# A hand-written order of 994 named operations is replaced by another order of the same operations (attention into a Hyena convolution, one core)

## The chip, the cores and the metric

The kernel runs on one core of one Trainium2 chip. The metric is the device time of one execution in microseconds (us), the median of several runs. TensorE (PE) does the matmuls, VectorE (DVE), ScalarE (ACT) and GpSimd (POOL) the rest; SyncE (SP) issues most of the transfers.

## The reference

Four batches, eight heads, 768 positions, head size 64. Three heads attend causally over everything; the other five see only the first 4 keys and the last 64. The attention's output, 768 x 512 for each batch, is projected to three parts; the middle one is convolved over the sequence with a filter (a circular convolution through a real FFT), multiplied by the other two, and projected once more.

```python
a = softmax(where(mask, q @ k.T / 8, -1e9))        # per batch and head
x = (a @ v) laid out as (4, 768, 512)
x1, x2, x3 = split(x @ w_proj, 3)                  # each (4, 768, 512)
x2_conv = irfft(rfft(x2) * rfft(filter_fft))       # over the 768 positions
return (x1 * x2_conv * x3) @ w_out
```

## The kernel before

The heads are taken in 16 pairs, n = 0 to 15, four for each batch b. All intermediate results stay in SBUF; the Fourier transforms are matmuls with tables of cosines and sines that the kernel makes at its start. Every step is a small function with a name, and the whole program is written out in one string, FAST: the functions are called in the order in which their names stand there. A scheduler does not move anything. So FAST fixes the order of the instructions on every engine; each engine works through its own list, and waits where data is missing.

A word of FAST is a name, then (for some) `/v`, `/s` or `/p`, the engine that does it (VectorE, ScalarE, GpSimd), then (for TensorE's) `@0` to `@3`, which of four PSUM buffers of two banks it writes:

```python
for word in FAST.split():
    name, _, slot = word.partition("@")
    name, _, eng = name.partition("/")
    now.update(slot=slot, engine=eng)
    ops[name]()
```

The names that matter here, with their lines:

- For a pair n: `lq`, `lk`, `lv` load q, k and v (L905, L927); `cq`, `ck` or, from pair 8 on, `cqk` cast to bf16 (L535 on VectorE, L537 on GpSimd, L541 on ScalarE); `T` transposes q and k into `qkT`, on TensorE for pairs 0 to 7 (L952, with the eviction `E`) and by a DMA that SyncE issues from pair 8 on (L962); `ks` copies the sink keys into the windowed heads' rows.
- `sc` are the scores (L990; contraction over the 64 rows of one head), `sb` adds masks in PSUM for the first four pairs (L1001), `ex` the exponentials on ScalarE (L1007), `mk` masks afterwards, `at` attention times v (L1050), `rec` and `nm` the normalisation on VectorE (L1056, L1067). `tn`/`te` transpose the result on TensorE (L1123) for pairs 0 to 10; from 11 on a DMA does it (L1132).
- `fd`, `fe`, `fA`, `fS`, `fb`, `fr` add and subtract the attention's thirds and halves (L544, L1095), `W` is the first half of the Fourier transform (L1103 to L1111) with its eviction `We`.
- For a batch b: `X` projects in the frequency domain (L1154), `Xe` evicts, `pa`, `pb`, `pc` multiply with the filter's spectrum, `c` is the inverse transform (L1227), `cv` its butterflies (L1238), `x1` and `x3` the two other projections (L1189), `g` and `y` the gating, `o` the output projection (L1262; the last tile in halves at L1257), `oe` its eviction, `st` the store.
- Once: `lfilt` loads the filter (L776, a DMA that GpSimd issues), `lw` and `lwo` the weights (L784, L789), `fold0` and `fold1` fold the filter (L793, L797), `F` transforms it (L805), `H` scales its spectrum out of PSUM.
- At the end: `chk` compares the head pattern with the expected one, `gd0` to `gd4` check on all rows that the softmax sums are sane, with one 1-column matmul, `gd3` (L669), and write one number, `other` (L674). The last line of the program reads `other` on all engines and branches to a general version if it isn't zero. `rest` is eight matmuls whose result nobody uses (L586). `late` is a two-element copy of the last output tile (L579).

The transfers have queues: SyncE issues its DMAs one after the other in FAST's order, and stops at one whose buffer or data isn't ready; GpSimd does the same with `lfilt`, `lw` and `lwo` between its computing instructions.

Of the kernel before, what the change touches and what calls it, by code (L numbers as in the profile page):

```python
# [64 lines left out]
ck1/p blank2@3 ones0 E0.0/v cq1/p btab lq3 gs1/v gs0/p sc0.0@0 sc0.5@2 gc/p cq2/p sc0.2@3 sb0.5 sb0.0 ck2/p ex0.5
sb0.2 kz0/v T1.1@1 gs2/p T1.0 E1.0/v sc0.4@2 ex0.2 sb0.4 ex0.0 blank1@3 sc0.1@3 E1.1/v sc0.3@0 ones2 lk3 sb0.3 ex0.4
lv2 cv0/p T2.0@1 lv3 sb0.1 kz2/p ex0.3 ex0.1 T2.1 gr0/v ones1 sc1.1@2 sb1.1 sc1.0@0 lk5 E2.1/v ex1.1 ck3/p gm0.2
sb1.0 cq3/p E2.0/s at0.0@3 at0.1 ks1/v lq5 gm1.2 sc2.1@2 Gk0 sc2.0@1 lfilt ex1.0 gm1.1 gm0.1 sb2.0 sb2.1 Gt0@0 rec0
cv1/s nm0/v ex2.0 lw1.1 Ge0/v Gt1@3 sc1.2@1 ex2.1 ks2/s vs1/v Gh0 sb1.2 vx1/s sc2.4@0 ex1.2 T3.0@2 T3.1 lq4 Ge1/v lk4
fd0/v E3.0/v lw1.0 ex2.4 lq6 sc2.3@3 at1.1@1 fe0/v sc2.2@0 at1.0 E3.1/v rec1 sb2.2 nm1/v ex2.3 W0.1@3 cv2/s cv3/p  # L70
vx3/s ex2.2 fe1/v tn0@2 W0.0 te0/s sc3.1@1 sb3.1 vx2/v fd1/v at2.0@0 ck5/p vs2/s sc3.0@2 at2.1 We0/v lv4 cq5/s ks3/s
T5.1@3 cq4/p sb3.0 T5.0 ex3.1 sc3.2@1 sb3.2 rec2 nm2/v fe2/p E5.0/v ck4/p E5.1/v ex3.0 Gh1 W1.0@0 lv5 ex3.2 T4.0@2
E4.0/s W1.1 tn2@1 lq7 vs3/v tn1@3 We1/s T4.1 te2/v sc5.0@1 sc5.1@0 lk6 te1/v at3.1@3 fold1 at3.0 E4.1/s fold0 rec3
# [15 lines left out]
x11.0.1@2 fr6 x11.0.0 T9 oe0.3/s at8.0@1 at8.1 lq11 fS7/v fA7/v oe0.1/s fr7 xs1.0/s chk cv9/v vx9/v sc9.1@0 fb6/p
fb7/v rec8 T10 lv10 nm8/v fe8/p sc9.0@3 x11.3.1@2 x11.3.0 W7.1@1 ex9.1 W7.0 W6.0@0 fd8/p ks9/p ex9.0 xs1.3/v W6.1  # L90
sc10.4@3 sc10.3@2 cqk11/p We6/v mk9.1 vs9/s We7/s sc10.0@1 lv11 ex10.4 ex10.3 sc9.2@3 mk9.0 ex9.2 X1.1.1@0 mk9.2 T11
tn8@2 X1.1.0 fS8/v ex10.0 Xe1.1/s X1.2.0@3 at9.1@1 te8/s at9.0 sc10.1@0 ks10/p X1.2.1 fA8/v ex10.1 Xe1.2/s sc11.0@2
rec9 sc11.1@0 cv10/v cv11/p nm9/v st0.1 x31.0.1@1 mk10.1 lk12 ex11.0 fd9/p ex11.1 x31.0.0 X1.0.1@3 lq12 sw1.1 lv13
ks11/v pa1.1/p sc10.2@2 vx10/s sc11.2@0 X1.0.0 g1.0 sw1.0 vs10/v vs11/v ex10.2 x11.2.0@1 pb1.1/v fe9/v lq14 Xe1.0/s
mr10 fb8/v mk10.0 fS9/v mk10.2 x11.2.1 o0.4.0@2 mk11.1 ex11.2 tn9@3 xs1.2/s at10.0@0 at10.1 mk11.0 lq13 mk11.2 fA9/v
x11.1.0@1 x11.1.1 o0.5.0 o0.4.1 o0.5.1 fb9/p vx11/s rec10 cqk12/s nm10/v at11.0@0 at11.1 fr9 te9/s fr8 fd10/p
x31.1.0@3 T12 oe0.5/s W9.1@2 W9.0 xs1.1/s pb1.2/v x31.1.1 rec11 nm11/v tn10@1 pc1.1/v We9/s W8.1@0 tn11 W8.0 te10/s
g1.1 pa1.0/v sc12.1@2 pa1.2/v sc12.4@3 x31.2.1@1 x31.2.0 We8/s sc12.0@0 fe10/v pc1.2/v fe11/p ex12.1 x12.0.0@2 g1.2
fS10/p fA10/p lk13 ex12.4 x12.0.1 ex12.0 x32.0.0@3 pb1.0/v lv12 fb10/p pc1.0/v xs2.0/s sc12.5@1 sc12.2@0 fd11/v
sc12.3@2 x32.0.1 ex12.5 c1.0.0@1 c1.0.1 ex12.2 fr10 fA11/v lq15 fS11/v W10.1@0 W10.0 ex12.3 fr11 c1.1.0@2 c1.1.1  # L100
fb11/p g2.0 ce1.0/s c1.2.0@3 We10/s ce1.1/s W11.0@0 cv1.0.1 cv13/p cv1.0.0 mk12.1 cv1.1.0 cv1.1.1 c1.3.1@1 cqk13/s
W11.1 c1.3.0 y1.1/v y1.0/v ce1.3/v lk14 We11/s c1.2.1 ce1.2/s cv1.3.0 X2.1.0@2 lk15 T13 cv1.3.1 cqk14/s cv1.2.1
cv12/s X2.0.0@0 X2.1.1 mk12.0 X2.0.1 x31.3.0@1 T14 mk12.2 Xe2.1/s x31.3.1 Xe2.0/s cv1.2.0 y1.3/v sc13.1@3 vs13/s
ex13.1 sc13.0@2 g1.3 cqk15/p at12.1@0 at12.0 pa2.0/p sc14.1@1 rec12 sc14.0@3 ex13.0 nm12/v vx13/s X2.2.0@2 y1.2/v
ks13/s X2.2.1 pb2.0/v o1.1.0@0 ex14.1 pa2.1/v T15 lv15 mk13.1 o1.1.1 ex14.0 sc13.2@1 sc15.0@3 mk13.0 pc2.0/v ks14/p
Xe2.2/s fe12/v ex13.2 sc15.1@2 mk13.2 o1.0.0 st0.5 ex15.0 o1.0.1 x12.3.0@1 pa2.2/v x12.3.1 pb2.1/v at13.1@3 ex15.1
at13.0 ks15/p tn12 oe1.1/s fd12/v rec13 xs2.3/s lv14 exp0 o1.4.0@2 o1.5.0 fS12/v sc14.4@0 nm13/v sw2.1 fA12/v
sc15.2@1 fe13/v sc14.3@3 fd13/v st0.3 ex14.4 sc14.2@0 ex15.2 o1.4.1 ex14.3 o1.5.1 x12.2.1@1 mk14.1 fS13/v fr12 ex14.2
# [1290 lines left out]
```

## Time and profile before

| | |
|---|---|
| median of 3 runs | 183.8 us (183.39 to 184.66) |
| span of the profiled execution | 182.1 us |
| what lies around the span, by the median | 1.7 us |
| TensorE busy | 172.8 us (95%) |
| VectorE busy | 149.8 us (82%) |
| ScalarE busy | 145.3 us (80%) |
| GpSimd busy | 77.5 us (43%) |
| DMA | 33.8 MB, 186 GB/s on average |

The profile's span begins with the first instruction and ends with the last. "Busy" for TensorE is the time in which at least one matmul is in flight; a matmul that starts a little late because its operands came late still counts as busy. The profiled execution has no time of its own beside its span: the 1.7 us is the median of the runs less the span.

### The profile page before, as it was taken

What the parts mean: (1) busy time and instruction counts of PE and PEld (TensorE: products, weight loads), DVE (VectorE), ACT (ScalarE), POOL (GpSimd) and SP (SyncE); (2) the same over time, 40 slices, a digit from 0 to 9 for tenths busy, and PEclk for the clock granted to TensorE, in tenths of its full rate; (3) what the DMA queues carried; (4) which work ended last, traced back from release to release, by engine and by line L of the source; (5) the groups of instructions that cost most, each with busy time, mean ns of one, the idle gap of its engine ahead of it and who ended that gap; (6) DMA issues with size and microseconds to landing.
All of it is one profiled execution on the core that took longest, in us unless ns stands there. A gap on an engine that the chain in (4) does not pass through costs nothing.

```text
span 182.1 us, 4374 instructions
## 1 busy us (share of the span) xinstructions
PE 172.8 (95%) x1684; PEld 103.6 (57%) x1700; DVE 149.8 (82%) x298; ACT 145.3 (80%) x196; POOL 77.5 (43%) x94
## 2 busy tenths in 40 slices
...
GB/s 159 356 203 287 294 257 200 204 290 230 232 224 166 184 228 198 116 214 142 265 217 200 150 231 166 123 208 243 228 153 112 184 0 0 58 2 119 127 277 184
DMA packets 78396, 33.83 MB, mean 186 GB/s; under 512 B 67618, under 2 KB 74786, under 8 KB 78370
## 3 DMA queue, kind: packets, MB, share of 16 engines
...
q14 instruction: 12, 0.10, 0.2%
...
## 4 chain that ended last, share of the span: by engine, by line
PE 82%; DVE 8%; ACT 4%; DMA 3%; issue 1%
PE f_x_ps L1189 23%; PE f_X_ps L1154 12%; PE f_out_ps L1262 10%; PE f_c_ps L1227 9%; PE f_sc L990 8%; PE f_att L1050 7%; DMA f_qkT<-f_qk_bf 3%; PE f_qkT_ps L952 2%; PE f_sc L1001 2%; PE warm L454 2%; PE f_xt_ps L1123 2%; ACT f_pT L1007 1%; DVE f_HAB L691 1%; PE f_W_ps L1103 1%; PE f_W_ps L1105 1%
## 5 line engine op out<-in xcount | busy, mean ns | idle before, releaser
L1007 ACT ACTIVATE f_pT<-f_sc 128x1024 bf16<-128x1024 f32 (+3 forms) x68 | 58.5, 914 | 3.6 <-PE f_sc L990 2.0
L1189 PE MATMUL f_x_ps<-f_xT,f_wproj 128*128 128x384 bf16 x256 | 46.9, 326 | 0.0
L1189 PEld LDWEIGHTS <-f_wproj 128*128 128x128 bf16 x256 | 23.9, 98 | 17.4 <-issue 1.6
L990 PE MATMUL f_sc<-f_qkT 64*128 64x128 bf16 (+3 forms) x328 | 20.9, 242 | 2.4 <-DMA f_qkT<-f_qk_bf 1.4
L1154 PE MATMUL f_X_ps<-f_wproj,f_xh 128*128 128x512 bf16 x90 | 22.1, 379 | 0.6 <-issue 0.2
L544 POOL TENSOR_TENSOR f_fo<-f_attn 128x384 bf16<-128x384 bf16 x15 | 14.6, 990 | 18.4 <-DVE f_attn L1067 17.3
L1262 PE MATMUL f_out_ps<-f_wout,f_gy 128*128 128x512 bf16 x86 | 22.0, 379 | 0.3
L990 PEld LDWEIGHTS <-f_qkT 64*128 64x128 bf16 x328 | 11.4, 94 | 13.0 <-issue 7.9
L1238 DVE TENSOR_TENSOR turns<-angle,f_c_ps 128x384 bf16<-128x384 f32 x32 | 16.3, 550 | 2.6 <-ACT angle L541 1.3
L1227 PE MATMUL f_c_ps<-f_Gi,f_P 128*128 128x384 bf16 x96 | 18.2, 326 | 0.1
L1050 PEld LDWEIGHTS <-f_pT 128*128 128x128 bf16 x472 | 16.2, 97 | 2.4 <-issue 0.4
L1050 PE MATMUL f_att<-f_v_aug,f_pT 128*128 128x65 bf16 x392 | 17.0, 193 | 0.0
L541 ACT COPY f_o<-f_out_ps 128x1024 f32<-128x1024 f32 (+2 forms) x15 | 12.1, 818 | 6.2 <-PE f_out_ps L1262 5.1
L541 ACT CAST f_X<-f_X_ps 128x1024 bf16<-128x1024 f32 x12 | 12.1, 1016 | 4.9 <-PE f_X_ps L1154 4.9
L1067 DVE TENSOR_TENSOR f_attn<-f_att,f_recs 128x768 bf16<-128x768 f32 x16 | 15.1, 951 | 0.6
L544 POOL TENSOR_TENSOR f_P<-f_X,f_HAB 128x1024 bf16<-128x1024 bf16 x4 | 8.9, 2215 | 14.5 <-ACT f_X L541 14.5
L544 POOL TENSOR_TENSOR f_gy<-turns,f_gy 128x768 bf16<-128x768 bf16 x5 | 8.5, 1710 | 14.6 <-DVE turns L1238 14.6
L1154 PEld LDWEIGHTS <-f_xh 128*128 128x128 bf16 x96 | 8.9, 97 | 10.2 <-issue 0.5
L1262 PEld LDWEIGHTS <-f_gy 128*128 128x128 bf16 x92 | 8.5, 98 | 8.8 <-POOL f_uv L544 0.4
L541 ACT COPY angle<-f_c_ps 128x384 f32<-128x384 f32 x15 | 7.2, 478 | 7.7 <-PE f_c_ps L1227 5.4
L1227 PEld LDWEIGHTS <-f_P 128*128 128x128 bf16 x96 | 9.1, 98 | 6.0 <-issue 0.2
L537 POOL CAST f_qk_bf<-qk_ahead 128x768 bf16<-128x768 f32 (+1 forms) x9 | 8.0, 900 | 8.7 <-DMA qk_ahead<-in_k_dram 3.4
...
## 6 DMA issues: line engine op xcount, KB each, us to landing
...
```

What stands on the lines that cost most here:

```text
L537: nc.gpsimd.tensor_copy(out=out, in_=in_)
L541: nc.scalar.copy(out=out, in_=in_)
L544: (nc.gpsimd if now["engine"] == "p" else nc.vector).tensor_tensor(out, a, b, op)
L990: nc.tensor.matmul(sc[:, bank, col:col + 128 * cnt], lhsT=keys, rhs=qkT(n)[rows, 0, 128 * i:128 * (i + cnt)], start=(col == 0 or not biase ...
L1007: nc.scalar.activation(out=pT(n)[:, c, :, 0:w], in_=held[f"sc.{n}.{c}"][:, :, 0:w], func=AF.Exp, scale=SCALE)
L1050: nc.tensor.matmul(att[:, hh, 65 * i:65 * i + 65], lhsT=pT(n)[:, c, bank, col:col + 128], rhs=values, start=(z == 0), stop=(z == len(here) ...
L1067: nc.vector.tensor_mul(attn(n).rearrange("p i hh d -> p hh i d"), rows[:, :, :, 0:64], recs()[:, n][:, :, :, None].to_broadcast([128, 2, N ...
L1154: nc.tensor.matmul(ps[:, u, :], lhsT=xh(b)[:, cc, chain, 128 * part:128 * part + 128], rhs=wproj()[:, cc, DM:2 * DM], start=(cc == 0), sto ...
L1189: nc.tensor.matmul(ps[:, s, 0:HS], lhsT=wproj()[:, cc, part * DM + cb * 128:part * DM + (cb + 1) * 128], rhs=xT(b)[:, cc, s * HS:s * HS + HS],
L1227: nc.tensor.matmul(ps[:, r, 0:HS], lhsT=P(b)[:, t, u, ch], rhs=Gi()[:, tile_no], start=(m == 0), stop=(m == 2))
L1238: fn(conv[:, half * HS:half * HS + HS], held[f"evs.{b}.{cb}"], held[f"c_ps.{b}.{cb}"][:, 1, 0:HS])
L1262: nc.tensor.matmul(ps[:, i % 2, :], lhsT=gy(b)[:, cb, i * 128:(i + 1) * 128], rhs=wout()[:, cb, :], start=(cb == 0), stop=(cb == NC - 1))
```

## The change

FAST is replaced by another sequence of the same 994 words' names. No function, tile, constant or matmul is added or taken away. Three things differ: the order of the names, the engine letters of some of them, and the PSUM buffer numbers of some. The first line of the table, before and after, and the last:

```diff
-mtab3 lq2 lk2 wrap0 size blank3@0 sin1 ck0/v lv0 T0.1@1 E0.1/s kz1/v sin2 cq0/p cos2 blank0@2 alt cos1 T0.0 lv1 gr1/s
+ck0/s wrap0 mtab3 blank2@0 size lq2 cos2 blank3@0 sin2 T0.1@2 E0.1/v sin1 blank1@3 cos1 alt gc/v gr0/v ones2 btab
...
-o3.2.0@3 o3.2.1 o3.3.0@2 oe3.1/s o3.3.1 oe3.4/v st3.0/v oe3.2/s oe3.3/s o3.5.1@1 st3.4/v st3.1/v oe3.6/s o3.5.0@0
-oe3.5/s st3.6/s st3.2/v st3.3/v st3.5/v rest@3 late
+oe3.4/v st3.6/s st3.4/v oe3.2/v st3.2/v oe3.5/s o3.3.0@0 o3.3.1 gd0 gd1 gd2 late oe3.3/s st3.5/v rest@2 chk st3.3/v
+gd3@1 gd4
```

Counted by kind, the engine letters move `ce` (inverse transform's eviction) from 15 on ScalarE and 1 on VectorE to 10 and 6, `oe` from 15 and 1 to 12 and 4, `te` from 7 and 4 to 5 and 6, the copies `vx` from 8 on ScalarE to 4 (4 now on GpSimd), `cqk` from 6 on ScalarE to 4, and the casts `cv` of v from 7 on VectorE, 5 on GpSimd, 4 on ScalarE to 3, 10 and 3. The filter's `H` go from 4 on VectorE and 5 on ScalarE to 6 and 3. Of the casts of q and k in the first stage `cq1`, `ck1`, `ck3`, `cq3`, `cq4` go from GpSimd and `cq5` from ScalarE to VectorE. TensorE's list alternates between `sc` and other work 76 times before and 70 times after.

Three places, engine by engine. The first is GpSimd around the load of the filter (`f_filt`), some 17 to 24 us into the program. Before:

```order
L537 CAST f_v_aug_177<-f_v_f_0_139 128x12x64
L880 MEMSET f_v_x_270 64x520
L884 MEMSET f_v_aug_281 128x12
L537 CAST f_qk_bf_307<-qk_ahead_66 128x768 x2
L776 DMA f_filt<-in_moe_filter_fft_dram 128x6x512
L784 DMA f_wproj<-in_moe_w_proj_dram 64x4x512 x2
L537 CAST f_v_aug_177<-f_v_f_3_265 128x12x64
```

and after:

```order
L880 MEMSET f_v_x_418 64x520
L537 COPY f_qkT_292<-f_qkT_292 64x4x4
L776 DMA f_filt<-in_moe_filter_fft_dram 128x6x512
L537 COPY f_v_x_166<-f_v_aug_162 64x4x65
L537 CAST f_v_aug_194<-f_v_f_3_370 128x12x64
L537 COPY f_qkT_497<-f_qkT_497 128x4x4
L537 COPY f_v_x_418<-f_v_aug_194 4x520
L544 TENSOR_TENSOR f_fo_584<-f_attn_576 128x384
L537 CAST f_qk_bf_541<-qk_ahead_69 128x768
L784 DMA f_wproj<-in_moe_w_proj_dram 64x4x512 x2
```

The filter's load stood behind two casts of pair 3's q and k; it now stands behind the sink copy of pair 2 (`ks2`, the copy within `f_qkT_292`), which must wait until TensorE has made the scores `sc2.0` and `sc2.1`. The first two weight loads (`lw1.0`, `lw1.1`) stood right behind the filter's and now come six instructions later.

The second is SyncE's list around the transpose of pair 12 (`f_qkT_12`), about 98 us into the program. Before and after:

```order
L1179 DMA f_Xw_1_1719<-f_X_1_2_1671 64x1024
L908 DMA f_qk_f32_14_1762<-in_q_dram 128x6x64 x2
L908 DMA qk_ahead1_69<-in_q_dram 128x6x64 x2
L962 DMA_TRANSPOSE f_qkT_12_1885<-f_qk_bf_12_1848 128x12x128
L1132 DMA_TRANSPOSE f_xT_2_1645<-f_attn_11_1905 128x6x128
```

```order
L927 DMA f_v_f32_13_1799<-in_v_dram 128x6x64 x2
L962 DMA_TRANSPOSE f_qkT_12_1822<-f_qk_bf_12_1765 128x12x128
L908 DMA qk_ahead0_66<-in_q_dram 128x6x64 x2
L908 DMA qk_ahead1_69<-in_q_dram 128x6x64 x2
L1132 DMA_TRANSPOSE f_xT_2_1664<-f_attn_11_1904 128x6x128
```

The load of pair 13's q (the row into `qk_ahead1`) stood in front of this transpose; it now stands behind it, with pair 15's between. The cast that feeds the transpose (`cqk12`) goes from ScalarE to VectorE.

The third is the end of VectorE's list. Before and after, from the last gating on:

```order
L1219 TENSOR_TENSOR f_gy_2676<-turns,f_x_ps_3_2832 128x384
L674 TENSOR_SCALAR other<-f_rows_right,differ 1x1
L535 COPY f_o_2_2883<-f_out_ps_4_2855 128x512
L579 CAST f_sane<-f_o_2_2883 1x2
L1314 TENSOR_LOAD other
```

```order
L535 COPY f_o_1_2879<-f_out_ps_2_2862 128x512
L655 TENSOR_SCALAR f_sane<-f_recs 128x192
L660 SCALAR_TENSOR_TENSOR f_sane<-f_recs,f_sane 128x192
L665 TENSOR_REDUCE f_right<-f_sane 128x1
L579 CAST f_sane<-f_o_2_2874 1x2
L642 MEMSET want 1x8
L645 MEMSET want 1x1 x3
L646 TENSOR_SCALAR zeros<-flags 1x16
L648 TENSOR_TENSOR local<-zeros 1x8
L649 TENSOR_TENSOR differs<-local,want 1x8
L650 TENSOR_REDUCE differ<-differs 1x1
L674 TENSOR_SCALAR other<-f_rows_right,differ 1x1
```

The checks (`gd0` to `gd2`, `chk`, `gd4`) stood earlier in the program and `other` was written before the last output tiles; they now stand behind the last evictions. On TensorE `gd3`, whose result `gd4` reads, stood in front of batch 3's output projection; it now is the last matmul of all, behind the eight of `rest`.

More of the change, by code (lines that the diff above doesn't have):

```diff
@@ L63 @@
 FAST = """
-mtab3 lq2 lk2 wrap0 size blank3@0 sin1 ck0/v lv0 T0.1@1 E0.1/s kz1/v sin2 cq0/p cos2 blank0@2 alt cos1 T0.0 lv1 gr1/s
[L65 to L73, printed above, removed]
@@ L89 @@
[L89 to L98, printed above, removed]
@@ L99 @@
[L99 to L108, printed above, removed]
@@ L114 @@
-fS14/p fA14/p x32.3.1@0 cv2.0.0 x13.1.1@2 fA15/p ce2.2/s x13.1.0 g2.2 x32.3.0 xs3.1/s fr14 fb15/v y2.0/v fb14/v
-W14.0@3 W14.1 x13.0.1@2 We14/s cv2.2.0 fr15 x13.0.0 W15.0@3 W15.1 cv2.2.1 x33.0.1@1 We15/v x33.0.0 y2.2/p X3.2.1@3
-X3.2.0 xs3.0/s Xe3.2/s X3.1.1@2 y2.3/v g3.0 X3.1.0 X3.0.1@1 sw3.1 g2.3 Xe3.1/s sw3.0 X3.0.0 x13.2.1@0 pa3.1/v Xe3.0/s
-o2.1.0@3 x13.3.0@2 o2.0.0 pa3.2/p x33.2.0@1 x13.2.0 pb3.1/p x13.3.1 pb3.2/v gd0 pc3.2/v o2.1.1 xs3.2/s pa3.0/v
-pb3.0/v x33.2.1 x33.1.0@0 pc3.1/v o2.0.1 xs3.3/s g3.2 c3.0.0@2 pc3.0/p x33.1.1 c3.1.0@1 oe2.1/s ce3.0/s o2.4.0@3 g3.1
@@ new lines @@
+kz2/v cq0/s T0.0 E0.0/s lk2 sc0.3@0 ones1 sb0.3 sc0.2@1 ex0.3 gs1/p lv0 gs2/s ones0 gr1/v gm1.1 sc0.0@2 sb0.0 ck1/v
+sb0.2 blank0@0 T1.1@3 Gh0 cq1/v T1.0 gm1.2 ex0.2 sc0.5@0 sb0.5 ex0.0 sc0.1@1 sb0.1 ck2/p sc0.4@2 lk3 sb0.4 ex0.5
+E1.0/v E1.1/v T2.1@0 lv1 ex0.1 cq2/p T2.0 sc1.0@3 sc1.1@1 sb1.1 lq3 E2.1/v lq5 gm0.1 sb1.0 E2.0/v cv0/p ks1/v gm0.2
+ex0.4 lv2 at0.1@2 Gt1@0 at0.0 ex1.1 sc2.0@1 ex1.0 sc2.4@3 lv3 lq4 Ge1/s kz1/p rec0 nm0/v cv1/p vs1/v sc1.2@0 sb2.0
+sb1.2 lk5 gs0/s ck3/v ex2.4 Gt0@3 vx1/s kz0/p sc2.1@2 Ge0/v ex2.0 tn0@1 ks2/p sb2.1 ex1.2 te0/v sc2.3@3 fd0/v ex2.1
```

75 lines of the change are left out of this document (52 added, 23 removed).

## The prediction

> **What bounds the kernel now.** I read the page's busy line and chain first, then the stages, then the chain in order of time where a stage has idle TensorE time.
>
> ```profile
> PE 172.8 (95%) x1684; PEld 103.6 (57%) x1700; DVE 149.8 (82%) x298; ACT 145.3 (80%) x196; POOL 77.5 (43%) x94
> PE 82%; DVE 8%; ACT 4%; DMA 3%; issue 1%
> ```
>
> TensorE is busy for 95% of the span and makes 82% of the chain that ended last. Its matmuls are the same before and after. So an order can win only what TensorE waits, and that is little; it can lose much more. The stages (TensorE's column is the first) show where it waits:
>
> ```profile
> 10.00:15.00 5.00, 4.58 (x53) 2.65 (x52) 3.30 (x6) 5.00 (x7) 3.69 (x8) 1.00 1.02 225
> 20.00:25.00 5.00, 4.41 (x58) 2.73 (x55) 4.95 (x8) 4.90 (x8) 3.59 (x5) 1.00 1.06 317
> 35.00:40.00 5.00, 5.00 (x34) 2.48 (x34) 4.92 (x7) 4.89 (x9) 4.08 (x7) 1.00 0.94 264
> 100.00:105.00 5.00, 3.60 (x35) 2.39 (x33) 4.42 (x7) 3.77 (x5) 2.26 (x3) 1.00 1.09 155
> 150.00:155.00 5.00, 4.95 (x27) 2.46 (x26) 3.19 (x4) 1.51 (x3) 1.13 (x2) 1.00 0.00 0
> ```
>
> The granted clock is 1.00 in each of them, so its pauses have cost no clock yet. TensorE is idle for 0.42 and 0.59 us in the two early stages, where ScalarE (5.00, 4.90) or VectorE (4.95) is full, and for 1.40 us in the one at 100. From 105 on it has nearly everything. At 35 to 40 it looks full, but the chain says otherwise:
>
> ```profile
> 15.28 1.29 PE f_att L1050 x42
> ...
> 17.77 0.68 PE f_Gi_ps L766 x12
> ...
> 18.52 0.85 ACT f_pT L1007
> 19.37 0.62 DVE f_v_x L535
> ...
> 20.88 0.87 DVE f_qkT L535
> 21.75 1.23 DVE f_fo L544
> 22.98 0.87 DVE f_qkT L535
> ...
> 30.88 1.02 DVE f_xT L535 x2
> 31.90 0.86 DVE f_fold L797
> 32.76 0.87 DVE f_fold L793
> ...
> 35.03 1.12 DVE f_HAB L691
> ...
> 37.40 1.14 DVE f_HAB L691
> ```
>
> From 19.4 to 25 and from 31 to 40 us VectorE's list carries the chain: TensorE's work there is spread out at VectorE's pace. So the first 40 us are bound by ScalarE and VectorE together, the rest by TensorE.
>
> **The change part by part.**
>
> *The wait at 102 us.* SyncE's transposes of q and k for pair 12, and what followed:
>
> ```profile
> 95.51 0.98 PE f_att L1050 x32
> 96.48 1.30 PE f_x_ps L1189 x8
> ...
> 98.13 5.49 DMA f_qkT<-f_qk_bf
> ...
> 103.66 0.61 PE f_sc L990 x6
> 104.27 1.41 PE f_x_ps L1189 x8
> ...
> 106.00 2.06 PE f_x_ps L1189 x12
> ```
>
> ```profile
> PE f_sc L990 <- DMA f_qkT<-f_qk_bf: 1.4, 1, 1.4
> ```
>
> ```profile
> 95.75 2.27 SPq L908 DMA_DIRECT2D qk_ahead<-in_q_dram  x2
> 98.13 2.18 SPq L962 DMA_TRANSPOSE f_qkT<-f_qk_bf  x1
> 100.82 1.21 SPq L1132 DMA_TRANSPOSE f_xT<-f_attn  x1
> ```
>
> The transpose went out when SyncE had issued pair 13's load (95.75 + 2.27 = 98.02), and landed 5.49 us later; TensorE waited 1.40 us. In the new order that load stands behind the transpose, and TensorE does at10.0, at11.0, at11.1 and half a projection (four matmuls of x31.1) more between the transpose's place and the scores: 43 attention matmuls at 0.98 / 32 and half of 1.30, so 1.32 + 0.65 = 1.97 us, more than the 1.40. The wait goes. What is late next is the other transpose, `f_xT`, on which x12.0 rests: by the group of its kind it lands after 3.8 us, at 104.6, and x12.0 began at 106.00; without the 1.40 it would have begun at 104.6. In the new order it has pair 13's and pair 15's loads in front. Cost between 0 and 1.4 (the whole gain); I take 0.2, since x31.1 and x31.2 (1.30 each for eight), W9, W8, tn10 and three scores again lie between pair 11's attention and x12.0, some 5 us with the normalisation and the transpose running beside them. **Sum -1.2 us.**
>
> ```profile
> f_xT<-f_attn SPq DMA_TRANSPOSE x5, 3.8
> ```
>
> *Fewer turns between scores and other work.* Eight projection matmuls take 1.30 us (at 96.48), right behind scores 1.41 (at 104.27): a turn costs 0.11. There are 76 before and 70 after: 6 x 0.11 = **-0.6 us** (between 0, if they fall where TensorE waits anyway, and -0.7).
>
> *The filter.* Its load and what it moves:
>
> ```profile
> 18.86 1.04 POOL L776 DMA_DIRECT2D f_filt<-in_moe_filter_fft_dram  x1
> ```
>
> ```profile
> f_filt<-in_moe_filter_fft_dram POOLq DMA_DIRECT2D x1, 768.0 KB, 12.7
> L535 DVE CAST f_qk_bf<-qk_ahead 128x768 bf16<-128x768 f32 x4 | 2.3, 574 | 0.0
> ```
>
> It landed at 18.86 + 12.7 = 31.56, and VectorE folded from 31.90 on: no slack. Now it stands behind the sink copy of pair 2, which waits for sc2.0 and sc2.1, and these come behind attention 0, sc2.4, sc1.2, four mask matmuls and both table transposes. Attention 0 ended at 15.28 + 1.29 = 16.6. The listed work is about 2.7 us, an estimate from that chain: 18 table transposes at 0.68 for 12 are 1.0, and sc2.0, sc2.4, sc1.2, sc2.1 with the masks the rest. So the copy ends at about 19.6 and the filter lands at 32.3. `fold0` (0.87) then ends at 33.2, and F2.0 can start 0.4 us behind today's F2.1 (which started at the end of the first fold, 32.76). All of F, H and X of batch 0 follow. **+0.5 us**; bounds -1.0 (if the load lands sooner and VectorE has its two evictions, 1.02 at 30.88, behind it) and +2.5 (below).
>
> *Load between the engines in the first 40 us.* VectorE takes over six casts (0.574 each, 3.4 us) and gives up one eviction (0.87): up to +2.6 us where it is full. ScalarE and GpSimd get lighter by as much, and TensorE's idle 0.42 and 0.59 could shrink, -1.0. I take 0, because each of the two full engines has already shown its turn on the chain: what ScalarE gains at 18.5 VectorE asks for at 20.
>
> *The end.*
>
> ```profile
> 173.27 0.20 DVE L674 TENSOR_SCALAR other<-f_rows_right,differ 1x1 int32<-1x1 f32 x1
> ...
> 178.09 0.16 DVE L579 CAST f_sane<-f_o 1x2 bf16<-1x2 f32 x1 [3.17 <-ACT f_o L541]
> ```
>
> ```profile
> 176.77 0.87 PE f_out_ps L1257 x8
> 177.65 1.73 PE f_rest_ps L586 x8
> ```
>
> `other` was there at 173.47; at the end only the last stores, `late` (to 178.25) and the branch stood between the last useful matmul (177.64) and the span's end: 182.1 - 177.6 = 4.5 us, `rest` hidden beside them. Now `gd3` stands behind `rest` and `other` behind `gd3`: 1.73 + about 0.1 + 0.2 = 2.0 us behind the last useful matmul, where `late` used to be over after 0.6. All engines read `other` before they branch. Bounds: 0, if the last store's landing ends the program anyway, and 2.0 - 0.6 = +1.4, if nothing does. I take **+1.0**, nearer the upper end, because the row of the store shows only its issue, at 178.08, and the closing of the program follows the branch. `chk` and `gd0` to `gd2`, ten small VectorE steps, hide beside `rest`.
>
> **Sum**: -1.2 - 0.6 + 0.5 + 0 + 1.0 = -0.3 us, a span of 181.8. With the 1.7 us around the span (183.8 less 182.1): **183.5 us**.
>
> **The rivals.**
>
> *Faster: the first 40 us open up.* If ScalarE's and VectorE's new shares fit, the 1.0 us of visible idle time goes, and the filter's 0.5 us too, because F stays covered by attention 3. For it: VectorE was held for 1.23 us by a half-width add at 21.75 that takes 0.36 elsewhere, while GpSimd worked beside it:
>
> ```profile
> 21.68 1.30 DVE L544 TENSOR_TENSOR f_fo<-f_attn 128x384 bf16<-128x384 bf16 x1
> ...
> 25.02 0.36 DVE L544 TENSOR_TENSOR f_fo<-f_attn 128x384 bf16<-128x384 bf16 x1
> ```
>
> ```profile
> 21.92 0.84 POOL L537 CAST f_qk_bf<-f_qk_f 128x768 bf16<-128x768 f32 x1
> ```
>
> That is 0.9 us on the chain, and the new order means to avoid it. 183.5 - 1.0 - 0.5 - 0.9 = 181.1; with half of the idle time, 181.6. Against it: VectorE's greater load.
>
> *Slower: the filter comes late.* The same three rows show that VectorE and GpSimd hold each other up. The new order puts four casts on VectorE (ck3, cq3, cv2, cq5) just where GpSimd makes the filter's transfer. If each holds it for its 0.574 us, the filter lands 2.3 us later, at 34.6; fold, F, H and X are all behind it, and no other work of TensorE's is left there but W2 and W3. It decides from about 33 us on; then each us is one of the total. 183.5 + 2.5 = 186.0. The Trainium skill ("SBUF — State Buffer", section "SBUF: two separate sides") says that a DMA from GpSimd's queue has its descriptors written by GpSimd, and that these wait while VectorE runs an fp32 copy within SBUF that takes both of its ports. By that rule this rival would be the forecast; this trace shows the mutual hold for two computing instructions, but no row of it shows a DMA's descriptors held.
>
> *Nothing of what it says: one wait for another.* The wait at 102 goes, and `f_xT` of pair 11, or the transpose of pair 13, costs the 1.4 us instead: 183.5 + 1.2 = 184.7.
>
> **How the numbers follow.** A measurement of this kernel tells about 1% (1.8 us) from no change. Forecast 0.43 and the exchanged wait 0.10 both lie within 1%; faster 0.27 (181.6 is 1.2% under 183.8); slower 0.20 (186.0 is 1.2% over). The range runs from 181.2 to 186.0: it leaves out about a third of the faster case and half of the slower.
>
> **What would show it.** Right: no wait of `f_sc` on `f_qkT` near 100 us; the filter's issue at 19 to 20 us with VectorE's folds at 32 to 33; the chain's end going from `rest` through `gd3` to `other`, with 5.5 us from the last output matmul to the span's end. Wrong: folds before 31.5 or after 34; a new row that waits for a DMA; TensorE idle by more than 0.3 us in any stage behind 105; VectorE's adds beside GpSimd still at 1.3 us.

## The result, and the profile after

The changed kernel takes **195.75 us** (median of 4, 195.49 to 197.51) against 184.19 for before: a ratio of 1.067 (95% interval 1.059 to 1.075), 6.7% slower, where the prediction said 183.5 and at most 186.0. (Before itself moved between 181.95 and 187.87 us in later runs; the ratios leave out executions over 1.5% above the fastest of their kernel, so a ratio and the medians beside it can differ, and then the places in the traces decide.) The page of the profiled execution, span, busy time and the shares of the chain (which could be followed back only to 72 us, so its shares don't add up to 100%):

```profile
span 193.6 us, 4402 instructions
...
PE 176.0 (91%) x1700; PEld 104.1 (54%) x1700; DVE 162.3 (84%) x313; ACT 136.8 (71%) x179; POOL 76.5 (39%) x96
...
PE 48%; DVE 4%; ACT 3%; issue 2%; DMA 1%; SPq 0%; DVEq 0%; ACTq 0%
```

The span is 11.5 us longer, VectorE is 12.5 us busier, ScalarE 8.5 less busy. The stages (TensorE's column first, as before):

```profile
10.00:15.00 5.00, 3.57 (x38) 1.79 (x35) 3.76 (x7) 4.33 (x7) 3.08 (x4) 1.00 1.20 277
25.00:30.00 5.00, 3.90 (x68) 2.97 (x67) 3.59 (x10) 3.13 (x5) 1.95 (x5) 1.00 1.08 174
50.00:55.00 5.00, 4.12 (x91) 3.71 (x89) 3.97 (x8) 3.61 (x5) 3.57 (x3) 1.00 1.20 213
70.00:75.00 5.00, 3.64 (x44) 2.24 (x42) 3.92 (x8) 3.49 (x6) 3.42 (x2) 1.00 1.14 185
100.00:105.00 5.00, 5.00 (x33) 2.75 (x31) 4.96 (x13) 3.72 (x6) 0.00 (x0) 1.00 0.86 179
185.00:190.00 5.00, 1.49 (x8) 0.51 (x6) 1.09 (x11) 0.34 (x1) 0.00 (x0) 1.00 0.41 145
```

The idle 1.40 us at 100 is gone, as forecast. New holes stand at 10, 25, 50 and 70 us, with the clock at 1.00, and the end is longer. No engine is full in the stages with holes: TensorE stands there at one instruction whose input or bank isn't ready. What TensorE waited for (in all, times, longest):

```profile
PE f_c_ps L1227 <- ACT angle L541: 1.9, 3, 0.8
PE f_qkT_ps L952 <- ACT f_qkT L541: 1.9, 3, 1.2
...
PE f_sc L990 <- ACT f_qkT L541: 0.9, 1, 0.9
PE f_qkT_ps L952 <- DVE f_qk_bf L535: 0.7, 1, 0.7
PE f_blank_ps L593 <- ACT f_pT L1007: 0.7, 1, 0.7
```

To see where the time goes I counted TensorE's useful work, every matmul but the blank ones, in units in which 512 columns are 0.213 us (those of `rest` follow each other every 0.216), timed by the weight loads, which the traces have in full, about 163 us in both kernels, and noted when each trace reached so many microseconds of it. The table gives before's time, and in each column how many microseconds later the profiled execution of a kernel came there (the kernels follow below):

| useful work | before at | after | open_before2 | mid_before | ce_behind | t6_early | open_blanks | open_letters |
|---|---|---|---|---|---|---|---|---|
| 0 | 5.53 | 0.69 | -0.02 | -0.02 | 0.08 | 0.10 | -0.29 | 0.68 |
| 5 | 13.66 | 2.20 | -0.02 | 0.47 | 1.97 | 2.03 | 0.74 | 5.60 |
| 20 | 30.79 | 2.72 | -0.66 | 1.50 | 2.48 | 2.54 | 1.31 | 11.21 |
| 35 | 45.75 | 3.01 | 0.19 | 2.51 | 2.77 | 2.84 | 1.61 | 12.03 |
| 40 | 50.78 | 4.50 | 2.96 | 2.51 | 4.26 | 3.88 | 3.10 | 13.65 |
| 60 | 71.43 | 6.43 | 4.89 | 2.71 | 4.84 | 5.81 | 5.03 | 15.58 |
| 90 | 101.55 | 7.36 | 5.81 | 3.72 | 5.77 | 6.73 | 5.96 | 16.50 |
| 95 | 108.00 | 5.97 | 4.42 | 2.33 | 4.38 | 5.34 | 4.57 | 15.11 |
| 100 | 112.69 | 6.19 | 5.91 | 3.82 | 5.87 | 6.84 | 6.06 | 15.34 |
| 125 | 138.21 | 6.08 | 5.51 | 3.74 | 5.66 | 6.33 | 5.62 | 15.49 |
| 160 | 173.80 | 7.03 | 6.62 | 4.69 | 6.01 | 7.53 | 6.76 | 16.45 |

After loses 3.0 us in the opening, 3.4 in batch 0's convolution (35 to 60 us of work), 0.9 up to 90, wins 1.4 at pair 12's transpose, loses 1.1 in what follows: **7.0**. The other **4.5** come behind the last useful matmul. Each column is one execution, and the opening differs between executions: at 35 us of work the five traces with before's order up to there (before, mid_before, tail_late, t12_early, before_plus) lie between -0.7 and +2.6 us of the first column, the five with after's opening unchanged (after, ce_behind, t6_early, mask_behind, tail_early) between 2.8 and 3.3. So after's is later in every pair, but the 3.0 is the difference of two executions. The end of after, and the two rows that lie first in the opening:

```profile
11.50 0.59 PE L593 MATMUL f_blank_ps<-blank 128*128 128x512 bf16 x2 [0.70 <-ACT f_pT L1007]
...
13.15 0.51 PE L952 MATMUL f_qkT_ps<-identity,f_qk_bf 128*128 128x128 bf16 x6 [0.73 <-DVE f_qk_bf L535]
...
184.51 1.89 PE L586 MATMUL f_rest_ps<-blank 128*128 128x512 bf16 x8
...
186.33 0.17 PE L669 MATMUL f_rows_right<-f_v_aug,f_right 128*1 128x1 bf16 x1
...
186.53 0.20 DVE L674 TENSOR_SCALAR other<-f_rows_right,differ 1x1 int32<-1x1 f32 x1 [0.38 <-PE f_rows_right L669]
```

`other` is written at 186.74, and the span ends 6.9 us later, at 193.6.

### The profile page after: what moved, and what is told of

It reads as the page before. It is cut to its first block, busy times and chain, and to the rows that moved or that the text cites. A ratio compares the mean times of both kernels' runs of the same rounds, so it can differ in the third digit from the quotient of the medians.

```text
span 193.6 us, 4402 instructions
## 1 busy us (share of the span) xinstructions
PE 176.0 (91%) x1700; PEld 104.1 (54%) x1700; DVE 162.3 (84%) x313; ACT 136.8 (71%) x179; POOL 76.5 (39%) x96
## 3 DMA queue, kind: packets, MB, share of 16 engines
q0 software_dynamic: 2944, 2.88, 10.2%
## 4 chain that ended last, share of the span: by engine, by line
PE 48%; DVE 4%; ACT 3%; issue 2%; DMA 1%; SPq 0%; DVEq 0%; ACTq 0%
PE f_x_ps L1189 15%; PE f_out_ps L1262 8%; PE f_X_ps L1154 7%; PE f_c_ps L1227 6%; PE f_sc L990 3%; PE f_att L1050 3%; DVE turns L1238 2%; ACT f_pT L1007 1%; DMA out_dram<-f_o 1%; PE f_W_ps L1103 1%; PE f_W_ps L1105 1%; DVE f_pT L1025 1%; ACT f_o L541 1%; PE f_rest_ps L586 1%; PE f_W_ps L1107 1%
## 5 line engine op out<-in xcount | busy, mean ns | idle before, releaser
L1189 PE MATMUL f_x_ps<-f_xT,f_wproj 128*128 128x384 bf16 x256 | 47.4, 326 | 0.1
L1262 PE MATMUL f_out_ps<-f_wout,f_gy 128*128 128x512 bf16 x92 | 23.0, 379 | 0.3 <-DVE f_gy L1219 0.3
L1154 PE MATMUL f_X_ps<-f_wproj,f_xh 128*128 128x512 bf16 x96 | 22.7, 379 | 0.1
L541 ACT COPY f_o<-f_out_ps 128x1024 f32<-128x1024 f32 (+2 forms) x12 | 10.5, 886 | 11.4 <-PE f_out_ps L1262 4.8
L544 POOL TENSOR_TENSOR f_gy<-turns,f_gy 128x768 bf16<-128x768 bf16 x6 | 10.2, 1700 | 20.8 <-DVE turns L1238 20.8
L541 ACT CAST f_X<-f_X_ps 128x1024 bf16<-128x1024 f32 x11 | 11.0, 1012 | 5.9 <-PE f_X_ps L1154 5.7
L541 ACT CAST f_xh<-f_W_ps 128x768 bf16<-128x768 f32 x14 | 11.2, 800 | 5.4 <-PE f_W_ps L1107 4.2
L537 POOL CAST f_v_aug<-f_v_f 128x768 bf16<-128x768 f32 x10 | 9.2, 918 | 8.4 <-DMA f_v_f<-in_v_dram 8.2
L1025 DVE TENSOR_TENSOR f_pT<-f_pT,mtab 128x1024 bf16<-128x1024 bf16 (+1 forms) x18 | 12.3, 691 | 0.0
L544 POOL TENSOR_TENSOR f_fo<-f_attn 128x384 bf16<-128x384 bf16 x9 | 9.1, 1023 | 7.0 <-DVE f_attn L1067 6.9
```

Of the source, the lines that this page charges most:

```text
L541: nc.scalar.copy(out=out, in_=in_)
L544: (nc.gpsimd if now["engine"] == "p" else nc.vector).tensor_tensor(out, a, b, op)
L1025: nc.vector.tensor_mul(some, some, tab.to_broadcast([128, 2, cols, 128]))
L1154: nc.tensor.matmul(ps[:, u, :], lhsT=xh(b)[:, cc, chain, 128 * part:128 * part + 128], rhs=wproj()[:, cc, DM:2 * DM], start=(cc == 0), sto ...
L1189: nc.tensor.matmul(ps[:, s, 0:HS], lhsT=wproj()[:, cc, part * DM + cb * 128:part * DM + (cb + 1) * 128], rhs=xT(b)[:, cc, s * HS:s * HS + HS],
L1262: nc.tensor.matmul(ps[:, i % 2, :], lhsT=gy(b)[:, cb, i * 128:(i + 1) * 128], rhs=wout()[:, cb, :], start=(cb == 0), stop=(cb == NC - 1))
```

## The experiments

Each kernel is one of the two with a few words of FAST moved. Times are medians; the ratio is to the kernel before on the same chip.

| kernel | us | before beside it | ratio (95%) |
|---|---|---|---|
| open_before | 197.74 | 185.02 | 1.065 (1.056 to 1.075) |
| mid_before | 191.19 | 185.02 | 1.030 (1.021 to 1.038) |
| tail_late (from before) | 188.08 | 185.02 | 1.013 (1.000 to 1.026) |
| tail_early | 192.35 | 185.02 | 1.036 (1.027 to 1.045) |
| open_casts | 195.15 | 183.89 | 1.061 (1.053 to 1.070) |
| ce_behind | 193.78 | 183.89 | 1.056 (1.047 to 1.064) |
| t6_early | 196.07 | 183.89 | 1.067 (1.060 to 1.075) |
| t12_early (from before) | 185.32 | 183.89 | 1.012 (1.005 to 1.019) |
| open_before2 | 194.85 | 184.37 | 1.058 (1.049 to 1.068) |
| mask_behind | 195.04 | 184.37 | 1.059 (1.050 to 1.067) |
| after_fixed | 189.49 | 184.95 | 1.039 (1.027 to 1.050) |
| before_plus (from before) | 184.26 | 184.95 | 1.004 (0.999 to 1.010) |
| open_letters | 204.9 | 184.07 | 1.116 (1.097 to 1.134) |
| open_blanks | 195.36 | 184.07 | 1.067 (1.057 to 1.077) |

### The end: tail_late and tail_early

```diff
 before -> tail_late
-... gd3@3 o3.0.0@2 o3.4.0@1 y3.3/v g3.3 gh o3.0.1 gd4 oe3.0/s ... rest@3 late
+... o3.0.0@2 o3.4.0@1 y3.3/v g3.3 gh o3.0.1 oe3.0/s ... rest@3 late gd3@1 gd4
```

> Before, with gd3 and gd4 alone moved to the very end, behind rest and late. Theory A, the program's closing needs `other` on GpSimd, which then runs 6.0 us of closing code of its own (in before it did that at 173.5 to 176.5, beside TensorE's work): `other` at 179.8, span 186.6, time 188.3 or +4.5. Theory of the prediction, only rest and gd3 are added to the end: `other` 1.4 to 2.0 us later than `late` was, 185.2 to 185.8.

```diff
 after -> tail_early
-... g3.0 ... y3.3/v gh ... gd0 gd1 gd2 late ... rest@2 chk st3.3/v gd3@1 gd4
+... gd0 gd1 gd2 chk g3.0 ... gd3@1 y3.3/v gd4 gh ... late ... rest@2 st3.3/v
```

> After, with gd0 to gd2 and chk moved ahead of g3.0 (where VectorE is idle for 2.3 us), gd3 ahead of y3.3 and gd4 behind it. Theory A: the closing code of GpSimd lies beside the last output stages, the end goes back to the last store (issued 185.4, some 3.8 us before the span's end in before): span 189.3, time 191.4 (-4.4, to -3.9 if gd3 and gd4 cost 0.3 on the way). Theory of the prediction (rest and gd3 only): -1.4 to -2.0, 193.8 to 194.4.

When the check value was written in tail_late, behind `rest`, and in tail_early, with its last store:

```profile
177.48 1.89 PE L586 MATMUL f_rest_ps<-blank 128*128 128x512 bf16 x8
...
179.50 0.21 DVE L674 TENSOR_SCALAR other<-f_rows_right,differ 1x1 int32<-1x1 f32 x1 [1.26 <-PE f_rows_right L669]
```

```profile
181.13 0.20 DVE L674 TENSOR_SCALAR other<-f_rows_right,differ 1x1 int32<-1x1 f32 x1
...
186.62 0.33 SPq L1295 DMA_DIRECT2D out_dram<-f_o  x1
```

tail_late reached the end of its useful work at the same moment as before (0.00), and its span is 185.8 for 182.1: 3.7 us for two words. (Its ratio, 1.013 with an interval that touches 1.000, says little by itself; the place in the trace does.) `other` to the span's end is 6.1 there (6.9 in after, 6.9 and 7.2 in open_before and mid_before). The records of GpSimd show where it goes: in after it reads `other` at 186.77, jumps to the closing code at 188.23, and its closing drain begins only at 191.94 and takes 0.81; Sync's is done at 189.08. In before the same steps lay at 173.50, 175.22 and 175.66, beside TensorE's last 4 us. In tail_early GpSimd's gap (183.09 to 185.68) lies beside the output stages again, and the span ends 1.5 us behind the last store's landing (189.16), as in before (180.38, 1.7). After's last store landed at 187.04; with 1.74 behind it, it would have ended at 188.8: by this working, an estimate, the place of the checks costs **4.8 us**. Between the last useful matmul and the span's end tail_early won 4.1 of them, and after_fixed (below) 3.5; in both the last store landed later behind that matmul than in after. That tail_early's median gains 3.4 and not 4.4 has its cause at 115 us (below), where its profiled execution lost 1.4. Theory A holds: the time goes into what follows `other`, not into `rest` and gd3. What GpSimd does there stays open. From its jump to its drain it takes 0.4 us in the four kernels with before's order elsewhere (before, tail_late, t12_early, before_plus) and 2.6 to 4.0 in the twelve others, whether all engines jump together (after 3.7, tail_late 0.4) or GpSimd jumps alone (tail_early 2.6, before 0.4). tail_late has 2.5 us behind the drain instead. The trace of after has transfers of the instruction queues at 188.5 to 190.2; no run here tests them.

### How far the loss is local: open_before, mid_before, open_before2

The first 202 or 414 words from before, and then after's words in after's order, without those done (banks renumbered where a bank was in use); in open_before2 `cv5/v` stands behind `H1.0/v` as well.

```diff
 after -> open_before, mid_before
-(after's words 1 to 198, 1 to 415)
+(before's words 1 to 202, 1 to 414)
 (the rest of after's words)
 open_before -> open_before2
-fe3/p cv5/v cq6/p ... H2.0/v ... H1.0/v mk4.1
+fe3/p cq6/p ... H2.0/v ... H1.0/v cv5/v mk4.1
```

> The first 202 operations in the sequence of before, all others in the sequence of after. In the trace of after TensorE reaches its 30th microsecond of useful matmul work 3.05 us later than in before, and its 163rd 7.0 us later. Theory A, the lag is made at a few places and stays: the 2.7 to 3.1 us of the opening go, 195.8 - 2.9 = 192.9 (192.4 to 193.4). Theory B, the new sequence asks VectorE for more (162.3 us busy for 149.8, and its engines hold each other up more), so that a lead is lost again in the stages behind: less than half of it stays, 194.4 or more.

> The first 414 operations in the sequence of before (up to about 73 us, all of batch 0's convolution), all others in the sequence of after. Theory A: the lag at that point, 6.3 us, goes; the rest (0.8 at 92 us, -1.4 at 102, some 0.9 from 148 on, and 4.5 behind the last useful matmul) stays: 195.8 - 6.3 = 189.5 (188.9 to 190.1). Theory B: less than half of it stays, 192.6 or more.

> The first 202 operations in the sequence of before and the others in that of after, as in open_before, but with VectorE's cast cv5 put behind H1.0. In open_before VectorE stood 2.4 us at cv5, which waited for pair 5's v (before's opening loads it later than after's), with all of H behind it, and the opening's lead of 3 us was lost between 35 and 50 us. Theory A, the opening's lag is made in the opening alone and that wait was the splice's own: the lead stays, TensorE is 2.4 to 3.1 us ahead of after at 35 us of work, and the time is 192.7 to 193.4. Theory B, VectorE's longer list behind the splice takes the lead back whatever the loads: less than 1.5 us ahead at 35 us of work, 194.3 or more.

open_before failed as a test: VectorE stood at cv5 for a load that before's opening issues later, and all that was won went with it. mid_before lies between the theories: the batch-0 stages cost nothing in it (2.51 at 35 us of work, 2.71 at 60), but its own opening came 2.5 late, and it lost 1.4 at the wait at 115 us (below), which after's own profile doesn't have. The late opening is before's in a bad execution. GpSimd's cast of pair 4's q waits for its load; in before's profiled execution and in mid_before's:

```profile
23.65 0.83 POOL L537 CAST f_qk_bf<-qk_ahead 128x768 bf16<-128x768 f32 x1 [0.88 <-DMA qk_ahead<-in_q_dram]
```

```profile
30.13 0.83 POOL L537 CAST f_qk_bf<-qk_ahead 128x768 bf16<-128x768 f32 x1 [6.26 <-DMA qk_ahead<-in_q_dram]
```

In the eight traces with that part of before's opening this cast begins between 23.65 and 30.21. So at 30 us of work the kernels with before's opening (open_before apart) lie between 40.1 and 43.3 us, those with after's sequence and engines, a few words moved, between 42.4 and 44.0. One reading is that the new order expects later loads and pays with a late opening in every execution; no run here tests it. In open_before2 the opening's lead over after holds up to 35 us of work (2.8 us, theory A); then 1.3 of it go again, while VectorE's masks stand beside GpSimd's casts, and 1.4 at 115 us, so that the time, 194.85, is theory B's:

```profile
43.27 2.90 DVE L1025 TENSOR_TENSOR f_pT<-f_pT,mtab 128x1024 bf16<-128x1024 bf16 x2
46.09 1.04 DVE L1017 TENSOR_TENSOR f_pT<-f_pT,mtab 128x512 bf16<-128x512 bf16 x1
47.05 0.55 DVE L1025 TENSOR_TENSOR f_pT<-f_pT,mtab 128x768 bf16<-128x768 bf16 x1
47.52 0.41 DVE L1017 TENSOR_TENSOR f_pT<-f_pT,mtab 128x512 bf16<-128x512 bf16 x1
```

The same mask of 512 columns takes 1.04 and 0.41. So not every loss is a wait: here an instruction of VectorE takes longer. That the longer masks make all of the 1.3 is argued, not shown.

### The opening: open_casts, open_letters, open_blanks

```diff
 after -> open_casts
-cq0/s ... ck1/v ... cq1/v
+cq0/p ... ck1/p ... cq1/p
 after -> open_letters: before's engine for 37 words, such as
-E0.1/v gc/v cq0/s E0.0/s ck1/v cq1/v E2.0/v ck3/v cq3/v E3.0/s
+E0.1/s gc/p cq0/p E0.0/v ck1/p cq1/p E2.0/s ck3/p cq3/p E3.0/v
 after -> open_blanks
-mtab3 blank2@0 size ... blank3@0 ... T0.0 E0.0/s ... sc0.2@1 ... blank0@0 T1.1@3
+mtab3 size ... blank3@0 ... T0.0 blank2@0 E0.0/s ... blank0@1 sc0.2@1 ... T1.1@3
```

> After, with three casts of the opening (cq0 from ScalarE, ck1 and cq1 from VectorE) back on GpSimd, where before had them. In after's trace TensorE stands at T1.0 until VectorE's cq1 ends at 13.10 (in before GpSimd's ended at 9.66), sc0.5 and ScalarE's exponentials wait behind it, and at 5 us of useful work TensorE is 2.2 us behind. Theory A, the engines of these casts make the opening late: TensorE's lag at 5 us of work falls from 2.2 to about 0.7, and the time to 194.3. Theory B, the places of TensorE's blank matmuls and evictions make it (T1.1 stands behind blank0, which waits for the first exponential): the lag stays above 1.5, time 195.0 to 195.8.

> The sequence of after, unchanged, but 37 operations of the opening on the engines that before gives them (before's letters for everything among its first 202 operations). Theory A, the new division of work among the engines makes the opening late (VectorE has 3.4 us more there, and small steps that stand between it and TensorE's banks): TensorE's lag at 20 to 30 us of work falls from 2.7 to 3.1 to under 1.0, the time by 2. Theory B, the order does (loads, blank matmuls and transposes issued where their input or their bank is not there yet): the lag stays at 2 or more, and with VectorE and ScalarE lists that fit the old order may grow.

> After, with two of TensorE's four blank matmul pairs moved: blank2 from the start to behind T0.0, blank0 from ahead of T1.1 to ahead of sc0.2 in another bank. In after the first transpose is 0.7 us later than in before, behind blank2 and blank3, and T1.1 stands 0.7 us behind blank0, which waits for the first exponential to leave its bank. Theory A, these places make a part of the lag: at 5 us of work it falls from 2.2 to 1.2 or less, and stays lower. Theory B, T1.0's wait for VectorE's cq1 (13.10) and the list behind it set the pace: less than 0.4 at 20 us of work.

open_casts won 1.0 us at 5 us of work and kept 0.4, hardly more than executions of the same opening differ by (2.8 to 3.3 above). open_letters refutes its theory A outright: before's engines under the new order put TensorE 12 us behind, since GpSimd then meets the casts of pair 0 only behind tables that wait for ScalarE; an order and its engines are one thing. open_blanks keeps 1.4 of the 3.0 us: two blank pairs ahead of the first transpose, and one pair in a bank that the first exponential still read, were 1.4 us of TensorE, more than executions differ by. That its median doesn't show it (195.36) comes again from 115 us, where it lost 1.5.

### Evictions and banks: ce_behind, t6_early

`c0.0.0` and `c0.0.1` write the two halves of one PSUM tile; `ce` copies the first half out.

```diff
 after -> ce_behind
-c0.0.0@3 nm6/v We5/s ce0.0/s c0.0.1 ... ce0.3/s cv0.0.0 tn6@1 c0.3.1 ... ce2.3/s c2.3.1
+c0.0.0@3 nm6/v We5/s c0.0.1 ce0.0/s ... cv0.0.0 tn6@1 c0.3.1 ce0.3/s ... c2.3.1 ce2.3/s
 after -> t6_early
-at5.0@3 lq8 Xe0.2/v H2.3 T6.1@0 Xe0.0/s at5.1 T6.0 E6.1/v
+T6.1@0 T6.0 at5.0@3 lq8 Xe0.2/v H2.3 Xe0.0/s at5.1 E6.1/v
```

> After, with three evictions (ce0.0, ce0.3, ce2.3: ScalarE's copy of the first half of a c_ps bank) put behind TensorE's second half of the same bank (c0.0.1, c0.3.1, c2.3.1) instead of ahead of it. Theory A, TensorE's second half waits for the copy, since it is a write to a tile that is being read, and the copy waits in ScalarE's queue: the three waits of 0.92, 0.77 and 0.73 us go, TensorE's lag at 65 us of work falls from 6.3 to 4.6 and the time by 2.4, to 193.4. Theory B, ScalarE and VectorE are behind at that point anyway, and TensorE waits for them a few steps later: less than 0.8, 195.0 or more.

> After, with TensorE's transposes T6.1 and T6.0 moved ahead of at5.0. In after T7.0 uses the PSUM bank of T6 and waits until ScalarE's E6.0 has left it (52.81), and E6.0 waits for VectorE's E6.1, which waits for T6.0. Theory A, this chain of one bank makes TensorE's 1.4 us of lag between 49 and 55 us: the chain begins about 0.9 earlier, the lag from 35 to 40 us of work falls from 1.5 to 0.6 or less, time 194.9. Theory B, the lag there is VectorE's load (it was 4.9 of 5 us busy from 35 to 50): nothing gained, 195.8.

After, in order of time: ScalarE is busy with We5, then copies, and TensorE's second half stands until the copy is done; and in ce_behind both halves run as one group:

```profile
70.79 0.65 PE L1227 MATMUL f_c_ps<-f_Gi,f_P 128*128 128x384 bf16 x3
70.96 0.80 ACT L541 CAST f_xh<-f_W_ps 128x768 bf16<-128x768 f32 x1
...
71.66 0.48 ACT L541 COPY angle<-f_c_ps 128x384 f32<-128x384 f32 x1
72.19 0.65 PE L1227 MATMUL f_c_ps<-f_Gi,f_P 128*128 128x384 bf16 x3 [0.75 <-ACT angle L541]
```

```profile
70.55 1.14 PE L1227 MATMUL f_c_ps<-f_Gi,f_P 128*128 128x384 bf16 x6
```

TensorE gained 1.35 us between 50 and 60 us of work and 0.6 between 125 and 135, 1.95 of the 2.4 expected, and the median is 2.0 below after's: theory A. t6_early gained 0.45 at its place, half of what its theory A said; its median, 196.07, shows no gain, since its profiled execution lost 1.4 at 115 us.

### The wait at 115 us: mask_behind

mk12.2 multiplies scores by a mask in SBUF; cqk13 is GpSimd's cast of pair 13.

```diff
 after -> mask_behind
-fr11 mk12.2 W10.1@3 ... g2.0 cv1.0.0 ... cqk13/p ... ce1.1/v y1.0/p
+fr11 W10.1@3 ... g2.0 cv1.0.0 ... cqk13/p ... ce1.1/v mk12.2 y1.0/p
```

> After, with VectorE's mask mk12.2 put behind ce1.1, so that VectorE's instructions beside GpSimd's cast cqk13 all read PSUM. In the profiled execution of after mk12.2 began at 116.57, 0.18 ahead of cqk13, and took 0.41; in five other kernels with the same order there cqk13 began first and TensorE lost 1.3 us at that point (in tail_early mk12.2 took 1.68, until cqk13's end, and g2.0, cv1.0 and W11 came behind it). Theory A, an instruction of VectorE with both operands in SBUF that starts second is held until GpSimd's ends, one that reads PSUM is not: no loss at 95 to 100 us of work in any execution, the time 0.9 to 1.4 below after's with its 1.3, 194.6 to 195.0. Theory B, cqk13 slows whatever VectorE does beside it: the loss stays, now at g2.0 and cv1.0, 195.6 to 196.2.

After, then tail_early (the same order there), then mask_behind:

```profile
116.57 0.41 DVE L1017 TENSOR_TENSOR f_pT<-f_pT,mtab 128x512 bf16<-128x512 bf16 x1
116.75 1.55 POOL L537 CAST f_qk_bf<-qk_ahead 128x1536 bf16<-128x1536 f32 x1 [0.39 <-DMA qk_ahead<-in_k_dram]
```

```profile
116.51 1.65 POOL L537 CAST f_qk_bf<-qk_ahead 128x1536 bf16<-128x1536 f32 x1
116.77 1.68 DVE L1017 TENSOR_TENSOR f_pT<-f_pT,mtab 128x512 bf16<-128x512 bf16 x1
...
119.36 0.32 PE L1227 MATMUL f_c_ps<-f_Gi,f_P 128*128 128x384 bf16 x1 [1.27 <-DVE f_gy L1208]
```

```profile
116.39 1.59 POOL L537 CAST f_qk_bf<-qk_ahead 128x1536 bf16<-128x1536 f32 x1
116.59 0.94 DVE L1208 TENSOR_TENSOR f_gy<-angle,f_x_ps 128x768 bf16<-128x768 bf16 x1
...
118.54 1.64 POOL L544 TENSOR_TENSOR f_gy<-turns,f_gy 128x768 bf16<-128x768 bf16 x1 [0.55 <-DVE turns L1238]
118.91 1.55 DVE L1017 TENSOR_TENSOR f_pT<-f_pT,mtab 128x512 bf16<-128x512 bf16 x1
```

A few tenths of a microsecond decide: the mask that begins first takes 0.41, the one that begins second takes until GpSimd is done. In ten traces with after's order there it took 0.41 twice (after, open_letters) and 1.68 eight times. In mask_behind VectorE's instruction beside the cast reads PSUM and takes its usual 0.94; the mask was held again (1.55), beside GpSimd's next instruction, where TensorE didn't need it. TensorE's loss at 95 to 100 us of work is gone, as theory A said. The median is 0.7 below after's, which the intervals of the two ratios don't tell apart. After's profiled execution doesn't have this loss, so it is no part of the 7.0 above.

### The one gain, alone: t12_early, before_plus; and all repairs: after_fixed

```diff
 before -> t12_early
-xs1.2/s at10.0@0 at10.1 mk11.0 lq13 ... cqk12/s ... T12
+cqk12/s xs1.2/s at10.0@0 at10.1 mk11.0 T12 lq13 ...
 before -> before_plus
-mk11.1 ... lq13 ... cqk12/s ... T12 ... (and) fe0/v sc2.2@0 at1.0 E3.1/v
+cqk12/v mk11.1 ... T12 lq13 ... (and) sc2.2@0 at1.0 E3.1/v fe0/v
```

> Before, with cqk12 ahead of xs1.2 on ScalarE and the transpose T12 ahead of lq13 in SyncE's queue. Theory A, the one wait that the change was forecast to take away: the transpose is issued at about 96.8 and lands at 102.3, TensorE's wait of 1.4 us falls below 0.2, ratio to before 0.992 to 0.994. Theory B, the wait is exchanged for another (f_xT of pair 11 for x12.0, or lq13 later for T13): 0.998 to 1.002.

> Before with two edits: pair 12's cast cqk12 on VectorE ahead of mk11.1 (where GpSimd is idle) with T12 ahead of lq13, as the new sequence has it; and VectorE's fe0, which was held for 0.96 us beside GpSimd's casts, put behind E3.1, which reads PSUM. Theory A: TensorE's wait of 1.4 at 102 us goes without xs1.2 coming later (that cost t12_early 1.1), and up to 0.8 in the opening: ratio to before 0.988 to 0.993. Theory B: VectorE, 0.96 us fuller at 95 to 100 us, hands the wait on to x12.0 or the convolution of batch 1, and the opening is bound by ScalarE: 0.997 to 1.002.

> After with all the repairs tried so far together: the opening of before (as in open_before2), ce0.0, ce0.3 and ce2.3 behind the second halves, T6 ahead of at5.0, mk12.2 behind ce1.1, and gd0 to gd4 and chk ahead of the last output stages (as in tail_early). Theory A, the losses are local and add up: opening 2.8 less the 1.3 that open_before2 lost again at VectorE's masks beside GpSimd's casts, evictions 1.95, T6 0.45, closing 4.8 (from `other` 186.7 and its 6.9 behind to 1.6 behind the last store): 195.5 - 1.5 - 1.95 - 0.45 - 4.8 = 186.8 (186.0 to 187.6), ratio to before 1.010 to 1.020. Theory B, behind each wait that goes stands another of like size: half of it, 191 or more.

In both, TensorE's wait for pair 12 is gone (1.4 and 1.3 us between 90 and 95 us of work). t12_early paid 1.1 of it ahead of that, at a projection whose bank waited for xs1.2, now behind the cast on ScalarE:

```profile
PE f_x_ps L1189 <- ACT angle L541: 1.0, 1, 1.0
```

before_plus paid 0.6 between 85 and 90 us of work. Neither is faster than before: t12_early's ratio is 1.012, with an interval wholly above 1, though its profiled execution is 0.7 us shorter than before's; before_plus can't be told from before. In before_plus VectorE's fe0, 1.30 us long in before, took 0.72, but the load of q came at 30.21 in its profiled execution and the opening 2.6 us late, so what fe0 is worth is not shown. after_fixed is 6.0 us below after's profiled execution, where 8.7 were expected: its copies and its mask won what they had won alone. The missing part by its trace: 0.7 in the opening (a bad execution again), 0.4 at T6, 0.65 between 95 and 125 us of work, and 1.3 at the end, where the last store landed 4.1 us behind the start of `rest` (2.5 in after). Both theories missed, A by 2.7 and B by 1.5; the losses are local, but do not quite add up. No kernel here beats before.

## Why the prediction was wrong, point by point

**The wait at 102 us: right.** No `f_sc` waits for `f_qkT` near 100 us, and TensorE wins 1.4 there (-1.2 said). One reading was off: pair 12's transpose was not held by pair 13's load alone. Its cast on ScalarE ended at the same 98.0, so moving the load alone would have won nothing; the new order also casts earlier, on VectorE.

```profile
96.56 1.47 ACT L541 CAST f_qk_bf<-qk_ahead 128x1536 bf16<-128x1536 f32 x1
```

**Fewer turns, -0.6: not shown either way.** All six lie in the first 35 us of work (36 turns before, 30 after), where the opening's loss covers them; behind that both orders have 40. Their price, 0.11 us a turn from one pair of rows, was not tested.

**The filter, +0.5: wrong in its steps, small in effect.** GpSimd's issue came at 22.31, not at 19.6, as its sink copy waited longer; the transfer landed 10.2 later, at 32.5, near the 32.3 said. The folds began at 34.87, past the 34 that the prediction had named as a sign of being wrong, because E5.1, We1, te2 and te1 stood ahead of them on VectorE:

```profile
21.75 0.20 POOL L537 COPY f_qkT<-f_qkT 64x16 bf16<-64x16 bf16 x1 [4.77 <-PE f_sc L990]
22.31 1.04 POOL L776 DMA_DIRECT2D f_filt<-in_moe_filter_fft_dram  x1 [0.37 <-issue]
...
34.87 0.95 DVE L793 TENSOR_TENSOR f_fold<-f_filt 128x1536 bf16<-128x1536 bf16 x1
```

The lag was 2.75 before that point and 3.05 behind it. The slower rival had the right sign for the wrong reason. Of the rule that I weighed there (the Trainium skill, "SBUF — State Buffer", section "SBUF: two separate sides") no run shows anything: the issue took 1.04 us, as in before.

**Load in the first 40 us, taken as 0: the first step that failed.** It measured +3.0 between the two profiled executions, beyond the upper bound of 2.6 (the spread of executions is told above). I had counted busy time moved between engines; what cost, as far as the runs show it, was where an in-order engine stands. 1.4 of it are two places of blank matmuls on TensorE (open_blanks). The cause of the other 1.6 stays open: neither the three casts nor the letters alone give them back.

**The middle, which had no term: the second.** That "the first 40 us are bound by ScalarE and VectorE together, the rest by TensorE" was read from before as if the new order kept it. I had written that an order can lose much more than it can win, and priced no loss. The runs show 1.95 us at three copies that stand ahead of the second half of their tile and 0.45 at T6's bank. In eight of ten traces, though not in after's own, 1.4 more go at a mask beside GpSimd's cast. The rest of the middle, some 3 us of losses, is in the table, but was not taken apart.

**The end, +1.0 of at most 1.4: the third, in its size.** `rest`, gd3, `other` was the right chain, 2.1 us behind the last useful matmul as worked out. The step "1.4 if nothing does" set nothing behind `other` but the branch; 6.1 to 7.2 us follow it, of which before hid the longest part. It cost 4.8 by the working above, of which tail_early and after_fixed won back 4.1 and 3.5.

**VectorE's adds beside GpSimd: the opposite.** The faster rival said that the new order avoids them. VectorE's two-operand instructions (TENSOR_TENSOR) that took over 0.2 us more than the shortest of their form, all beside GpSimd's work: 7 with 5.7 us over in before, 11 with 7.2 in after. How much of that TensorE felt was not measured.
